# A convolution in a transformed domain: where the second group of weights is prepared

## The chip, the cores and the metric

The kernel runs on one core of one Trainium2 chip. The metric is the device time of one execution in microseconds. Five runs of the kernel before gave 278.68, 279.45, 279.50, 281.03 and 282.76 us; their median, 279.5 us, is the time before.

## The reference

The reference is a circular convolution of an image of 224 x 224 pixels with 96 channels by a 7 x 7 filter with 96 input and 96 output channels, written with Fourier transforms:

```
x: (1, 224, 224, 96) bf16, w: (7, 7, 96, 96) bf16
wp = pad(w) to 224 x 224
Xf = rfft2(x over h, w);  Wf = rfft2(wp over h, w)
Yf = einsum('bhwi,hwio->bhwo', Xf, Wf)
y  = irfft2(Yf).astype(bf16)
```

The product over the channels for each output pixel is what has to be computed; the transforms of the reference are one way to it.

## The kernel before

**The work.** The image's rows are cut into 8 blocks of 28 rows, and within each block the kernel uses a short transform over 34 points (28 rows plus 6 of overlap), which has 17 frequencies. Along the width there is no transform but a direct convolution with 7 taps, folded into 10 (`NTAP`). The width is cut into 7 strips of 32 columns, `t` = 0 to 6. For each strip there are three stages: the forward transform of the image (tile `xf`, matmuls with the matrix `Fm`), a channel product for each frequency `s` (tile `WF` holds the transformed weights, tile `J` holds sums and differences of `xf`), and the transform back (`c_jobs`).

**The weights.** `WF` has one to three parts of 96 x 10 x 96 numbers for each frequency. They are made once, in six groups of frequencies, `PGRP = ((0, 2), (2, 5), (5, 8), ...)`: 12 jobs for a group, each some matmuls of the raw weights (tile `wq`) with a small matrix `Em`, and one copy from PSUM to `WF` (`evac`, by VectorE or ScalarE). For a frequency above 0 the matmuls make two parts, and a subtraction on VectorE, `diff(s)` in line 392, makes the third: it reads the outputs of all 12 jobs of its group.

The raw weights come from memory twice. The first copy fills every second partition of `wq`; the second copy, shifted by 48 output channels, fills the partitions between them. With the first copy alone a matmul makes one output channel (`first_prep`, line 345: 96 matmuls of 50 columns for group 0). With both, one matmul makes two output channels (`prep_jobs`, line 361: 48 matmuls of 120 columns for every other group). The loads of the second copy, `load_w(1, ...)` and `load_wl(1, ...)`, write partitions that the matmuls of the first kind read too, so they wait for the last of these.

**The order.** Every engine gets its instructions in the order in which the program lists them (`_Ordered`, line 77), and so do the transfers that the SP queue issues. The channel products run in rounds: `b_round(t, s, ...)` in line 518 is one frequency of one strip. A round has a first bank of matmuls, a place for other work called `mid`, a second bank of matmuls, subtractions for the tiles `J` in some rounds (`jit`, line 490, on VectorE), and another such place called `end`. These places are the half-rounds. `add(a, b, jobs)` in line 769 spreads a list of jobs evenly over the half-rounds `a` to `b - 1`, and `pace` takes from each list what is due, in the order in which the lists were added. Rounds 0 to 3 work on strip 0 alone, half-rounds 0 to 7; from round 4 on, strip 1 runs beside strip 0, four frequencies behind. Subtractions of `jit` stand in round 1 (frequencies 3 to 5 of strip 0), round 3 (0 to 2 of strip 1) and round 4 (6 to 8 of strip 0).

Before the rounds come the forward transform of the parts that are needed first, group 0's 12 jobs (lines 732 to 742), and the issue of the second weight copy (lines 743 and 744). In the rounds, group 1's 12 jobs all stand in half-round 3, its first `diff` behind them, and its other two in half-rounds 4 and 6. Group 2's jobs are spread over half-rounds 4 to 8. The first part of strip 1's forward transform (`f_jobs(1, 0)`, 8 jobs of 8 matmuls of 64 columns) is spread over half-rounds 0 to 2, its second part over half-rounds 7 to 13, and a rest of strip 0's over half-rounds 0 to 3.

PSUM has 8 banks here, and every job and every round's two banks take one in turn.

Of the kernel before, what the change touches and what calls it, by code (L numbers as in the profile page):

```python
# [25 lines left out]
NB = 8  # L26
POS = TW + HALO
NTAP = 10
TAPS = ((7, 8, 9, 6), (0, 2, 4, 6), (1, 3, 5))
NSLOT = 2 + 3 * (NS - 1)  # L30
PGRP = ((0, 2), (2, 5), (5, 8), (8, 11), (11, 14), (14, 17))
# [16 lines left out]
def slot(s, part):  # L48
    return part if s == 0 else 2 + 3 * (s - 1) + part
# [3 lines left out]
def kernel(  # L53
# [7 lines left out]
    _, H, W, C = x.shape  # L61
# [7 lines left out]
    PW2 = 2 * PW  # L69
# [28 lines left out]
    VE, SE, GE, TE, DE = (_Ordered(e) for e in (nc.vector, nc.scalar, nc.gpsimd, nc.tensor, nc.sync))  # L98
# [9 lines left out]
    def bank():  # L108
        return pools["psb"].tile([128, 512], F32, name="pb")

    load = {"v": 0.0, "a": 0.0, "p": 0.0}
# [3 lines left out]
    def apart(key, zone, r):  # L115
        for z, q in parts.setdefault(key, []):
            if z != zone and q.engine != r.ins.engine:
                tc.declare_no_dep(r.ins, q, reason="disjoint parts of one tile")
        parts[key].append((zone, r.ins))
        return r  # L120

    def evac(out_ap, in_ap, n):
        if tail[0]:
            return tail_evac(out_ap, in_ap, n)
        cv, ca = 180 + 1.0 * n, 160 + 0.85 * n
        for k in "va":
            load[k] = max(load[k], load["p"])
        if load["v"] + cv <= load["a"] + ca:
            load["v"] += cv
            return VE.tensor_copy(out=out_ap, in_=in_ap)  # L130
        load["a"] += ca
        return SE.copy(out=out_ap, in_=in_ap)

    def tail_evac(out_ap, in_ap, n):
        tail[0] += 1
        return VE.tensor_copy(out=out_ap, in_=in_ap) if tail[0] % 2 else SE.copy(out=out_ap, in_=in_ap)

    def dma(out_ap, in_ap):
        return DE.dma_start(out=out_ap, in_=in_ap)

    WF = cpool.tile([128, NSLOT, NTAP, C], BF16, name="WF")
# [18 lines left out]
    wqx = wtmp.tile([128, C - 1 + 127 * C + 1], BF16, name="wq")  # L160
    wq = wqx[0:PW2]
    WA = C * C
    WC = WA - C2
    WZ = WA // 3
    Em = wqx[0:PW2, WA:WA + 2 * NSLOT * NTAP].rearrange("p (h a t) -> p h a t", h=2, a=NSLOT)
# [26 lines left out]
    def load_w(h, cuts):  # L192
        for a, b in zip(cuts[:-1], cuts[1:]):
            wld.append(dma(wqx[h:2 * PW - 3 + h:2, a:b], wsrc[0:PW - 1, h * C2 + a:h * C2 + b]))

    def load_wl(h, n):
        wld.append(dma(wqx[2 * PW - 2 + h:2 * PW - 1 + h, 0:n], wsrc[PW - 1:PW, h * C2:h * C2 + n]))
# [7 lines left out]
    def warm(n):  # L205
        pwu = bank()
        for _ in range(n):
            TE.matmul(pwu[:].rearrange("p (a b) -> p a b", a=4), lhsT=wu[:, 0:128], rhs=wur, start=True, stop=True)
# [133 lines left out]

    g_fin = build_g(3)

    def first_prep():
        n = slot(PGRP[0][1], 0)
        q = n * NTAP
        wv = WF[0:C, 0:n].rearrange("i a t o -> i (a t) o")

        def mk_(o0):  # L350
            def f():
                pw = bank()
                pv_ = pw[:, 0:NB * q].rearrange("p (k q) -> p k q", q=q)
                for k in range(NB):
                    o = o0 + k
                    TE.matmul(pv_[:, k], lhsT=wqx[0:PW2 - 1, o:o + 127 * C + 1:C], rhs=Em[0:PW2 - 1, 0, 0:n].rearrange("p a t -> p (a t)"), start=True, stop=True)
                apart(("W", 0), o0, evac(wv[..., o0:o0 + NB], pv_[0:C].rearrange("i k q -> i q k"), NB * q))
            return f
        return [mk_(o0) for o0 in range(0, C, NB)]

# [44 lines left out]
    def new_xf(t, s0=0, s1=NS):  # L405
        xf = xf_bufs[t % 2]
        xf_tiles[t] = xf
        if t > 0:
            prev = xf_tiles[t - 1]
            for ph in range(2):  # L410
                o, i = (v[0:C, ph, :, s0:s1, p:p + HALO, :].rearrange("c r s w j -> c r s (w j)") for v, p in ((xf, 0), (prev, TW)))
                apart(("A", t), ("halo", s0), SE.copy(out=o, in_=i))
                load["a"] += 160 + 0.85 * 2 * (s1 - s0) * HALO * NJ
        return xf
# [35 lines left out]
    def then_load(f, t, jg):  # L450
        def g():
            f()
            if t < NT:
                load_x(t, jg)
        return g
# [11 lines left out]
    def f_jobs(t, part):  # L467
        s0, s1 = SH2[t][part], SH2[t][part + 1]
        n = 2 * (s1 - s0) * JG
        nr = -(-TW * n // 512)  # L470
        e = [-(-TW * i // nr) for i in range(nr + 1)]
        fv = Fm[:, :, s0:s1].rearrange("p r s j -> p r (s j)")

        def mk_(jg, a, b, ph):
            def f():
                pa = bank()
                load["p"] += max(26.0, 0.43 * n) * (b - a)
                for k in range(b - a):
                    i = 2 * (a + k) + ph
                    TE.matmul(pa[:, k * n:(k + 1) * n], lhsT=xbuf(t, jg)[:, i * C:i * C + 128], rhs=fv, start=True, stop=True)  # L480
                xo = xf_tiles[t][0:C, ph, :, s0:s1, HALO + a:HALO + b, jg * JG:(jg + 1) * JG]
                pi = pa[0:C, 0:(b - a) * n].rearrange("c (w r s j) -> c r s w j", r=2, s=s1 - s0, w=b - a)
                return apart(("A", t), (a, jg, ph, part), evac(xo, pi, (b - a) * n))
            return f
        return [[mk_(jg, a, b, ph) for a, b in zip(e[:-1], e[1:]) for ph in range(2)] for jg in range(2)]
# [232 lines left out]
    def queue_c(t):  # L718
        pend.extend((t, *k) for k in LT)
        pump()  # L720
# [5 lines left out]
    fj = [f_jobs(0, p) for p in range(2)]  # L726
# [2 lines left out]
            f()  # L729
    for _ in range(2):  # L730
        warm(5)
    pj = first_prep()
    for f in pj[:6]:
        f()
    for f in fj[0][1]:
# [4 lines left out]
        f()  # L740
    for f in pj[9:]:
        f()
    load_w(1, (0, WC))
    load_wl(1, WC)
    g_fin()
    stmp_cm.__exit__(None, None, None)
    yf_pool = ctx.enter_context(tc.tile_pool(name="yf", bufs=YBUF))
# [21 lines left out]
    def add(a, b, jobs):  # L769
        qs.append([a, b, jobs, len(jobs)])  # L770

    for gi in range(1, len(PGRP)):
        pj, dj = prep_jobs(gi)
        add(*((3, 4) if gi == 1 else (2 * PGRP[gi - 1][0], 2 * PGRP[gi - 1][1] - 1)), pj)
        for i, f in enumerate(dj):
            k = 2 * (PGRP[gi][0] + i) - (1 if gi == 1 and i == 0 else 2)
            add(k, k + 1, [f])
    for t in range(2):
        scr_tiles[t] = dr_pool.tile([TW, NJ, NS, 4 * C], BF16, name="scr")
# [9 lines left out]
    for r in range(NS + LAG):  # L789
        if r == 0:  # L790
            add(0, 4, fj[1][1])
        for p in range(2):
            if r == (0, 3)[p]:
                new_xf(1, SH2[1][p], SH2[1][p + 1])
                fj = f_jobs(1, p)
                if p == 1:
                    for jg in range(2):
                        fj[jg][-1] = then_load(fj[jg][-1], 2, jg)
                add(2 * r + p, 2 * r + (3, 8)[p], fj[0] + fj[1])
        for p in range(3):  # L800
            if r == (9, 14, 17)[p]:
                new_xf(2, SH2[2][p], SH2[2][p + 1])
                fj = f_jobs(2, p)
                if p == 2:
                    for jg in range(2):
                        fj[jg][-1] = then_load(fj[jg][-1], 3, jg)
                add(2 * r, 2 * r + (8, 7, 5)[p], fj[0] + fj[1])
        if r == PGRP[-2][1] + 1:
            assert not any(q[2] for q in qs if q[1] <= 2 * r)
            wtmp_cm.__exit__(None, None, None)  # L810
            t_pool = ctx.enter_context(tc.tile_pool(name="tt", bufs=NTT, side="right"))
            t2_pool = ctx.enter_context(tc.tile_pool(name="tt2", bufs=1, side="right"))
            yo_pool = ctx.enter_context(tc.tile_pool(name="yo", bufs=2, side="right"))
            g_pool = ctx.enter_context(tc.tile_pool(name="gp", bufs=1, side="right"))
            GA = g_pool.tile([KA, 4 * B], BF16, name="GA")
            GB = g_pool.tile([128, 2, 4 * B], BF16, name="GB")
            GE.memset(GA[:], 0.0)
            GE.memset(GB[:], 0.0)
        if r == NS + 3:
            queue_c(0)  # L820
        for t in range(2):
            s = r - LAG * t
            if not 0 <= s < NS:
                continue
            now = bursts.pop((r, t), ())
            now = jit(*now) if now else ()
            both = LAG <= r < NS
            b_round(t, s, fills(qs, 2 * r + (t if both else 0)), fills(qs, 2 * r + (t if both else 1)), False, now)
# [70 lines left out]
    for _ in range(WARM):  # L899
        TE.matmul(live[order[7]].rearrange("p (a b) -> p a b", a=3), lhsT=wu[:, 0:M4], rhs=wu[:].unsqueeze(1).to_broadcast([128, 3, 128]),  # L900
                  start=False, stop=False)
    LF = 4
    for i, (g, q) in enumerate(order):
# [3 lines left out]
        k = i + 8 - LF  # L907
        if 8 <= k < len(order):
            live[order[k]] = first(*order[k])
        if q % 2:  # L910
            w0, o0 = TL * 2 * TW + (q - 1) * 4, (q - 1) % 4 * 4 * C
# [33 lines left out]
```

## Time and profile before

| What | us |
|---|---|
| median of five runs | 279.5 |
| the profiled execution | 280.88 |
| its span in the profile | 279.2 |
| PE busy | 264.1 (95%) |
| DVE busy | 229.9 (82%) |
| ACT busy | 198.6 (71%) |
| matmuls that read `wq` (both kinds) | 336 |

PE is TensorE, PEld its weight loads, DVE VectorE, ACT ScalarE, POOL GpSimd, SP the queue that issues most transfers. The 1.7 us between the profiled execution and its span lie around the first and last instruction. PE counts as busy while a matmul's record lasts; records overlap, so the pace of a row of matmuls is its length, less the length of the last record, over the number less one. The granted clock is that of TensorE; 1.00 is full speed. The time of a line is measured from the start of the span, and "idle before" names what the engine waited for.

### The profile page before, as it was taken

To read this page: it belongs to the slowest core of one execution; us is meant where nothing else is said; L and a number is where in the kernel's file an instruction comes from. 1 tells how busy PE (TensorE), PEld (TensorE's weight loads), DVE (VectorE), ACT (ScalarE), POOL (GpSimd) and SP (SyncE) were. 2 spreads that over 40 slices of the span, in tenths; PEclk is the share of its full clock that TensorE was granted. 3 is DMA by queue.
4 is the path that set the end of the run, shared out by engine and by line. 5 is a ranking of instruction groups with operands and counts; after the bars stand their busy time and mean duration, and the time that the engine had idled before them with its cause. 6 is when DMAs were issued, how large, how long until landed. Compare 5 with 4: busy or idle time off the path is not lost.

```text
span 279.2 us, 12139 instructions
## 1 busy us (share of the span) xinstructions
PE 264.1 (95%) x5123; PEld 243.7 (87%) x5123; DVE 229.9 (82%) x470; ACT 198.6 (71%) x477; POOL 101.7 (36%) x152
## 2 busy tenths in 40 slices
PE   8989799989998999999999999999999999999964
PEld 3779699989998999898999999999999989989642
DVE  6865769998989979987986897789988889899823
ACT  6567777868784566898988869888888865552422
POOL 7820112254454456224234215222422333645100
PEclk9987979999999999999999999999999999999997
DMA  5975013231111279896978477875969843998675
GB/s 146 267 176 131 2 46 106 82 113 45 45 45 45 85 222 211 240 254 178 294 222 241 134 225 222 212 172 158 275 231 191 267 130 112 191 236 237 165 198 155
DMA packets 46355, 46.79 MB, mean 168 GB/s; under 512 B 35322, under 2 KB 37894, under 8 KB 46250
## 3 DMA queue, kind: packets, MB, share of 16 engines
q1 hardware_dynamic: 45836, 44.34, 57.9%
q0 software_dynamic: 464, 1.67, 1.7%
q8 instruction: 40, 0.66, 1.0%
q14 instruction: 15, 0.12, 0.2%
HBM read 24.66 MB, written 21.33 MB: 165 GB/s over the span
## 4 chain that ended last, share of the span: by engine, by line
PE 55%; DVE 21%; issue 7%; DMA 6%; ACT 5%; POOL 3%; SPq 1%; ACTq 0%; DVEq 0%
PE pb L87 55%; DVE J L87 8%; DVE WF L87 4%; DVE v L87 4%; POOL yf L87 3%; DMA WF<-in_x_dram 3%; ACT WF L87 3%; DMA tt<-scr 2%; DVE u L87 2%; DVE yf L87 1%; DMA xf<-scrl 1%; ACT wq L87 1%; SPq L87 1%; DVE yo L87 1%; ACT xf L87 1%
## 5 line engine op out<-in xcount | busy, mean ns | idle before, releaser
L87 PE MATMUL pb<-WF,J 96*128 96x96 bf16 x2898 | 168.7, 207 | 2.5 <-ACT WF L87 1.4
L87 PEld LDWEIGHTS <-J 96*128 96x128 bf16 x2898 | 142.7, 98 | 11.6 <-DVE J L87 1.7
L87 POOL TENSOR_TENSOR yf<-v,u 128x384 bf16<-128x384 f32 x85 | 84.6, 1012 | 147.1 <-issue 89.9
L87 ACT CAST xf<-pb 96x408 bf16<-96x408 f32 (+5 forms) x143 | 66.9, 488 | 8.9 <-PE pb L87 7.1
L87 PE MATMUL pb<-WF,xf 96*128 96x96 bf16 x952 | 61.7, 207 | 3.9 <-DVE WF L87 3.2
L87 DVE TENSOR_TENSOR J<-xf 96x1824 bf16<-96x1824 bf16 (+1 forms) x84 | 59.9, 752 | 0.0
L87 PEld LDWEIGHTS <-xf 96*128 96x128 bf16 x952 | 48.1, 98 | 4.9 <-issue 4.6
L87 PE MATMUL pb<-Fm,xn 118*128 118x136 bf16 (+4 forms) x576 | 44.9, 205 | 0.0
L87 ACT CAST WF<-pb 96x480 bf16<-96x480 f32 (+1 forms) x61 | 30.3, 559 | 5.9 <-PE pb L87 5.9
L87 PE MATMUL pb<-tt,Gm 102*84 102x384 bf16 (+1 forms) x132 | 33.6, 326 | 0.0
L87 PEld LDWEIGHTS <-xn 118*128 118x128 bf16 x576 | 29.6, 99 | 0.1
L87 ACT CAST yo<-pb 84x384 bf16<-84x384 f32 (+1 forms) x61 | 26.4, 481 | 4.1 <-PE pb L87 3.8
L87 ACT CAST J<-pb 84x384 bf16<-84x384 f32 (+1 forms) x61 | 26.5, 484 | 2.4 <-PE pb L87 2.4
L87 PE MATMUL pb<-wq 98*128 98x120 bf16 (+1 forms) x336 | 25.1, 228 | 0.0
L87 DVE TENSOR_TENSOR J<-J 96x912 bf16<-96x912 bf16 (+1 forms) x42 | 25.0, 594 | 0.0
L87 PEld LDWEIGHTS <-wq 98*128 98x128 bf16 (+1 forms) x336 | 23.0, 154 | 0.2
L87 DVE TENSOR_TENSOR WF<-WF 96x960 bf16<-96x960 bf16 x15 | 16.5, 1100 | 0.5 <-ACT xf L87 0.5
L87 PE MATMUL pb<-wu 128*128 128x512 bf16 (+3 forms) x57 | 15.4, 391 | 1.1 <-DVE wu L87 1.1
L87 DVE TENSOR_TENSOR yf<-v,u 128x384 bf16<-128x384 f32 x27 | 15.5, 572 | 0.9
L87 PEld LDWEIGHTS <-Gm 102*84 102x84 bf16 (+1 forms) x132 | 11.5, 117 | 1.7 <-issue 0.6
L87 PEld LDWEIGHTS <-wu 128*128 128x128 bf16 (+3 forms) x57 | 6.6, 117 | 6.5 <-issue 2.2
L87 DVE CAST xf<-pb 96x512 bf16<-96x512 f32 (+4 forms) x17 | 9.6, 590 | 2.8 <-PE pb L87 2.7
(395 smaller groups left out, 240.9 us busy)
## 6 DMA issues: line engine op xcount, KB each, us to landing
scr<-yf SPq DMA_DIRECT2D x30, 288.0 KB
xn<-in_x_dram SPq DMA_DIRECT2D x12, 672.0 KB
tt<-scr SPq DMA_DIRECT2D x24, 336.0 KB
out_dram<-yo SPq DMA_DIRECT2D x12, 252.0 KB
out_dram<-J SPq DMA_DIRECT2D x12, 252.0 KB
tt<-scr SPq DMA_DIRECT2D x6, 288.0 KB
scrl<-yf POOLq DMA_DIRECT2D x5, 288.0 KB, 5.0
WF<-in_x_dram SPq DMA_DIRECT2D x2, 672.0 KB
```

What stands on the lines that cost most here:

```text
L87: r = fn(*a, **k)
```

## The change

Group 1 is made from the single weight copy as well. `first_prep` becomes `single_prep(gi)`, which for group 1 takes the two computed parts of the three frequencies, 60 columns. Its 12 jobs have 8 matmuls and one copy to `WF` each; two stand before round 0, right behind group 0, and the other ten are spread over half-rounds 0 to 2. The loads of the second weight copy are issued behind the last of them. Group 1's first `diff` moves from half-round 3 to half-round 2. Group 2's jobs stand in half-rounds 6 to 8, four in each. The first part of strip 1's forward transform, with the copy of its halo columns, moves from half-rounds 0 to 2 to half-rounds 3 to 6, two jobs in each.

```
-    def first_prep():
-        n = slot(PGRP[0][1], 0)
-        q = n * NTAP
-        wv = WF[0:C, 0:n].rearrange("i a t o -> i (a t) o")
+    def single_prep(gi):
+        s0, s1 = PGRP[gi]
+        q = (slot(s1 - 1, 2) + 1 - slot(s0, 0)) * NTAP if gi == 0 else (s1 - s0) * 2 * NTAP
+        wv = WF[0:C, slot(s0, 0):slot(s1 - 1, 2) + 1]
+        ev = Em[0:PW2 - 1, 0, slot(s0, 0):slot(s1 - 1, 2) + 1]
+        if gi == 0:
+            ev = ev.rearrange("p a t -> p (a t)")
+        else:
+            ev = ev.rearrange("p (s r) t -> p s (r t)", r=3)[:, :, 0:2 * NTAP]
...
+                load["p"] += 60.0 * NB
                 for k in range(NB):
                     o = o0 + k
-                    TE.matmul(pv_[:, k], lhsT=wqx[0:PW2 - 1, o:o + 127 * C + 1:C], rhs=Em[0:PW2 - 1, 0, 0:n].rearrange("p a t -> p (a t)"), start=True, stop=True)
+                    TE.matmul(pv_[:, k], lhsT=wqx[0:PW2 - 1, o:o + 127 * C + 1:C], rhs=ev, start=True, stop=True)
...
-    pj = first_prep()
+    pj = single_prep(0)
+    p1 = single_prep(1)
...
-    load_w(1, (0, WC))
-    load_wl(1, WC)
+    for f in p1[:2]:
+        f()
+    p1_last = p1.pop()
+
+    def p1_end():
+        p1_last()
+        load_w(1, (0, WC))
+        load_wl(1, WC)
+    p1 = p1[2:] + [p1_end]
...
         pj, dj = prep_jobs(gi)
-        add(*((3, 4) if gi == 1 else (2 * PGRP[gi - 1][0], 2 * PGRP[gi - 1][1] - 1)), pj)
+        if gi == 1:
+            pj = p1
+        add(*((0, 3) if gi == 1 else (6, 9) if gi == 2 else (2 * PGRP[gi - 1][0], 2 * PGRP[gi - 1][1] - 1)), pj)
         for i, f in enumerate(dj):
-            k = 2 * (PGRP[gi][0] + i) - (1 if gi == 1 and i == 0 else 2)
+            k = 2 * (PGRP[gi][0] + i) - 2
             add(k, k + 1, [f])
...
-            if r == (0, 3)[p]:
+            if r == (1, 3)[p]:
...
-                add(2 * r + p, 2 * r + (3, 8)[p], fj[0] + fj[1])
+                add(2 * r + 1, 2 * r + (5, 8)[p], fj[0] + fj[1])
```

## The prediction

> **What bounds the kernel now.** I read the page first, then PE's timeline from 12 to 46 us, the stretch that the change touches, then the clock there window by window, then VectorE's timeline. The page:
>
> ```profile
> span 279.2 us, 12139 instructions
> ...
> PE 264.1 (95%) x5123; PEld 243.7 (87%) x5123; DVE 229.9 (82%) x470; ACT 198.6 (71%) x477; POOL 101.7 (36%) x152
> ...
> PEclk9987979999999999999999999999999999999997
> ```
>
> PE is busy nearly throughout, and behind 46 us it hardly rests: from 46 to 255 us it is busy for 206.0 of 209 us. So what PE gains or loses before 46 us reaches the end almost whole, unless VectorE (50.1 of 54 us busy from 46 to 100) holds it back; its lead has to be looked at too. The granted clock falls twice early. PE's timeline (start, length, group, idle before it):
>
> ```profile
> 17.40 3.10 PE L87 MATMUL pb<-wq 97*128 97x50 bf16 x48
> 21.08 0.80 PE L87 MATMUL pb<-WF,xf 96*128 96x96 bf16 x8 [0.58 <-ACT WF L87]
> ...
> 22.40 1.47 PE L87 MATMUL pb<-Fm,xn 118*128 118x64 bf16 x24
> 23.69 1.31 PE L87 MATMUL pb<-WF,J 96*128 96x96 bf16 x14
> ...
> 25.07 0.87 PE L87 MATMUL pb<-Fm,xn 118*128 118x64 bf16 x24
> ...
> 27.98 3.19 PE L87 MATMUL pb<-wq 98*128 98x120 bf16 x48
> ...
> 32.73 0.33 PE L87 MATMUL pb<-WF,J 96*128 96x96 bf16 x4 [1.40 <-ACT WF L87]
> ...
> 33.88 0.33 PE L87 MATMUL pb<-WF,xf 96*128 96x96 bf16 x4 [0.64 <-DVE WF L87]
> ```
>
> Group 1's 48 matmuls start without a wait, but behind them PE waits 1.40 us for their copies to `WF` and 0.64 us for the first `diff`. The clock (columns: busy time and count of PE, PEld, DVE, ACT, POOL, then PEclk):
>
> ```profile
> 14.81:18.22 3.41, 2.62 (x61) 2.54 (x60) 1.88 (x3) 1.98 (x5) 1.22 (x4) 1.00 1.00 235
> 18.22:21.63 3.41, 2.83 (x46) 2.74 (x45) 2.50 (x5) 2.94 (x8) 0.26 (x1) 0.50 0.21 62
> 21.63:25.05 3.42, 3.42 (x59) 3.42 (x57) 1.97 (x3) 1.79 (x5) 0.10 (x1) 0.50 0.96 241
> ...
> 31.87:35.28 3.41, 1.91 (x36) 1.83 (x37) 1.72 (x5) 1.91 (x5) 0.22 (x1) 1.00 0.04 10
> 35.28:38.70 3.42, 3.42 (x45) 3.42 (x43) 1.66 (x4) 2.59 (x7) 0.99 (x1) 0.50 0.01 2
> ```
>
> The clock is halved from 18.22 to 25.05 and from 35.28 to 38.70, always on a raster of 3.41 us. The window ahead of each fall held waits or many short matmuls. What counts seems to be the time in which columns stream: 512 columns take 216 ns (10 such matmuls in 2.32 us), so 0.42 ns a column. By that, 14.81 to 18.22 streamed 0.40 of the time and 31.87 to 35.28 about 0.45; both were followed by a fall. 11.40 to 14.81 streamed 0.54 and was not. At half clock, 18.22 to 21.63 streamed 0.60 and was not released, and 21.63 to 25.05 streamed all the time and was.
>
> **The change part by part.** Paces from the rows (length less last record, over number less one): 50 columns of `wq` 61 ns, 120 columns 63 ns, 64 columns of `xn` 30 ns (53 at half clock), 96 columns of `WF` 42 ns (79 at half clock), 72 columns 33 and 61 ns. The short `wq` matmuls kept 61 ns at both clocks.
>
> 1. PE's added work. 60 columns lie between the 50 and 120 that were measured, so 62 ns: 96 x 62 = 5.95 us for 48 x 63 = 3.02 us: **+2.9 us**, all on PE. The copies to `WF` stay 12 of 480 elements.
>    By the Trainium skill (TensorE: Matmul & The Clock Gate, Back-to-back issue gap) one matmul takes N/2.4 + 2.5 ns, 27.5 and 52.5 ns here, and this term would be +0.1 us; it says there that loads of weights add to this in a stream. The rows say that 50 and 120 columns cost the same.
> 2. Waits removed. Two jobs (16 matmuls, 1.0 us) fill the 0.58 us at 20.5: the last copies of group 0 end at 21.02, the jobs at about 21.3. Group 1's other jobs run beside rounds 0 and 1, one copy per 0.5 us shared by two engines that take 0.47 (ACT, 9 in 4.25 us) and 0.59 us (DVE, 3 in 1.77 us). The 1.40 and 0.64 us go: **-2.6 us** together.
> 3. What is late next. I followed the built order with these durations. PE reaches the end of round 0's first bank at 21.95, round 1 at 27.15, its last short matmul at 29.6, round 2 at 31.0, round 3 at 33.4. The first `diff` is ready at 30.85, before its use at 31.4. But on VectorE the J subtractions of round 1 (1.95 us by the row at 29.00 and the next) now stand behind it: 31.8 to 33.75. Behind them are a u and `diff(3)`, ready at 34.7, or at 35.2 if POOL's sum beside it slows it (0.65 us alone, 1.40 at 43.69 with POOL at work). PE wants it at 33.7: **+1.3 us** of new wait (bounds 1.0 to 1.5). Queued behind it are the rest of round 3 and group 2's jobs.
> 4. The second copy. Its loads move from 20.5 to 29.6 on SP, past nothing: SP's next transfer waits until 38.04 for a finished sum. Transfers ran until about 25.8, 5.3 us behind the issue; so it is there at 34.9 or up to a microsecond later, and half-round 6 wants it at 35.5. **+0.2 us** (bounds 0 and 3.5; the upper end from the first copy, issued from 3.12 and first read at 12.61, 9.5 us).
> 5. The moved transform. Its 8 jobs cost what they did; all 8 copies but one stand on ACT, which ends them at 34.85, then two halo copies, and round 3's scaled copy at 36.3. VectorE then has u, a `diff`, two copies to `WF`, one to `xf`, v, and the J subtractions for strip 1 from 39.5 to 41.5, against 41.56 to 43.5 before. Half-round 7 takes banks that u and these copies free, in time. `diff(5)` is ready at 43.9 instead of 45.1, PE's 0.46 us of wait there nearly goes (**-0.4 us**), and VectorE leads by 2 us. Cost of this move: nothing, with that lead as its cover; without it the 0.46 us stay.
> 6. First stretch of half clock. 22 matmuls of 96, 12 of 72 and 24 of 64 columns lost 22 x 37 + 12 x 28 + 24 x 23 ns = 1.7 us. Now 32 short matmuls, which lose nothing, fill 2.0 us of it: 13 of 96 and 12 of 72 lose 0.8 us. **-0.9 us**.
> 7. Second stretch. 30 matmuls of 96 columns and some 10 of `wq` lost 30 x 37 + 10 x 36 ns = 1.5 us. It followed the waits of part 2. In part 3 the wait is shorter, and the window streams some 0.5, which by the numbers above may go either way: **-1.5 us**, or 0.
>
> Sum: 2.9 - 2.6 + 1.3 + 0.2 - 0.4 - 0.9 - 1.5 = -1.0 us: a profiled execution of 279.9 instead of 280.88 us. Of that gain 2.4 us are clock. The five runs spread by 4.1 us and their median lies 1.4 us under the profiled execution, so the median one need not have had both falls. With all of the clock terms the median would be 278.5, with half of them 279.7; I take **279.0 us**, no change within 1%, which is about what a measurement of this kernel can tell from none.
>
> The Trainium skill (same page, What's actually happening) has a free-running window of 3413 ns, a fall after an idle one and a release after a busy one. The raster is in the trace; but the window ahead of 35.28 was not idle, PE worked for 1.91 us of it. By that rule the rival below could not happen.
>
> **The rivals.**
>
> *The clock stays halved (slower).* Short matmuls at half clock stream 50 of 62 ns. With 32 of them the window 21.63 to 25.05 streams 0.86 of the time, between 0.60 (not released) and 1.0 (released). If that is not enough, the next two windows with 24 each aren't either, and PE runs at half clock until 35.3: 61 matmuls of 96, 20 of 72 and 16 of 64 columns lose 61 x 37 + 20 x 28 + 16 x 23 ns = 3.2 us, of which the wait in part 3 hides 1.3. 279.0 + 1.9 = 280.9 us, and 282.2 without that cover. For it speaks the 0.60 row; against it that 0.86 is nearer to 1. It decides from the point at which a window with three in five matmuls short is not released.
>
> *The clock is released early and nothing waits (faster).* The two jobs at 20.3 raise the window 18.22 to 21.63 to about 0.73; if that releases at 21.63, 0.8 us more go, and if `diff(3)` is ready in time, 1.3 us more, with the 0.2 of the copy 2.3 in all: 278.5 - 2.3 = 276.2 us. Against it: J and `diff(3)` are in one queue.
>
> *The second copy lands late (slower).* If it takes the first copy's 9.5 us, PE waits 3.3 us more in half-round 6, and the clock falls behind it: 282.3 us. Against it: the first copy shared the queues with the image (DMA share 1.00 ahead of 18.22), this one has them alone (0.04 from 31.87 to 35.28).
>
> That the change doesn't do what it says is out: the built order has 16 short matmuls ahead of round 0, then 32, 24 and 24, and group 2 in three lots of 16 from half-round 6 on.
>
> **How the numbers follow.** Forecast 0.58, clock halved 0.20, early release 0.13, late copy 0.09. Half of the early release lies under 276.7, with 0.04 of the forecast: faster by over 1% 0.10. A third of the clock's rival and half of the copy's lie over 282.3: slower 0.11; within 1% 0.79. The range leaves out the lower part of the early release and the tops of the slower two: 276.5 to 281.8 us.
>
> **What would show it.** After: `wq` matmuls of 60 columns at about 62 ns; no wait for ACT's `WF` near 21 and 31 us; a wait for DVE's `WF` of some 1.3 us near 34; the first 120-column matmul near 35.5 to 36, with or without a wait for a DMA; full clock from 25 on. The prediction is wrong if short matmuls pace at half of 62 ns, if the clock is 0.50 past 25, or if the lead at 45 us is lost before 100 us in VectorE's queue.

## The result

Of the kernel before 71 runs now have a median of 279.27 us, of the changed one 36 runs have 278.85 us; the ratio is **0.9992, with a 95% interval of 0.9977 to 1.0007** (runs over 1.5% above a kernel's fastest are left out of every ratio here). The forecast was 279.0 us and no change within 1%. The time is right, the sum behind it only in part: its clock term for the first stretch failed, its new wait was too large, its price for the moved transform tells too little, and one of the rivals came about as well.

The profiled execution took 278.41 us, 2.5 us less than that of before. That is more than the change did. VectorE's last subtraction for `J` ahead of 97 us starts at 96.23 us instead of 96.94, so 0.7 us were won by then; the rest lies behind it. From 270 to 275 us the execution of before ran at a mean clock of 0.66, that of the changed kernel at 1.00.

The page of the changed kernel, with the same lines as before:

```profile
span 276.7 us, 12237 instructions
...
PE 265.6 (96%) x5171; PEld 245.4 (89%) x5171; DVE 229.8 (83%) x469; ACT 199.7 (72%) x478; POOL 101.8 (37%) x152
...
PEclk9996699999999999999999999999999999999998
```

PE has 48 matmuls more, and the clock has one low stretch ahead of 40 us instead of two. PE's timeline over the changed stretch:

```profile
17.09 4.06 PE L87 MATMUL pb<-wq 97*128 97x50 bf16 x64
...
21.32 2.13 PE L87 MATMUL pb<-wq 97*128 97x60 bf16 x32
23.28 0.90 PE L87 MATMUL pb<-Fm,WF 118*128 118x72 bf16 x12
23.98 1.31 PE L87 MATMUL pb<-WF,J 96*128 96x96 bf16 x14
25.10 1.64 PE L87 MATMUL pb<-wq 97*128 97x60 bf16 x24
...
28.36 1.65 PE L87 MATMUL pb<-wq 97*128 97x60 bf16 x24
...
35.90 0.33 PE L87 MATMUL pb<-WF,xf 96*128 96x96 bf16 x4 [0.32 <-DVE WF L87]
...
36.72 1.20 PE L87 MATMUL pb<-wq 98*128 98x120 bf16 x16 [0.19 <-DMA wq<-in_w_dram]
```

The three waits of before (0.58, 1.40 and 0.64 us) are gone; two small ones have come, for the second subtraction of group 1 (0.32 us) and for the second weight copy (0.19 us). The clock by windows of 3.41 us (busy time and count of PE, PEld, DVE, ACT, POOL, then the clock):

```profile
19.14:22.55 3.41, 3.41 (x63) 3.41 (x61) 2.20 (x4) 3.22 (x9) 0.38 (x1) 1.00 0.15 37
22.55:25.96 3.41, 3.41 (x56) 3.41 (x55) 1.78 (x3) 1.76 (x5) 0.00 (x0) 0.50 0.00 0
25.96:29.38 3.42, 3.42 (x54) 3.42 (x53) 1.02 (x4) 2.58 (x6) 0.00 (x0) 0.50 0.02 5
29.38:32.79 3.41, 3.41 (x58) 3.41 (x56) 2.70 (x6) 2.14 (x5) 0.00 (x0) 0.50 0.54 134
32.79:36.20 3.41, 3.09 (x83) 2.98 (x80) 3.41 (x6) 3.23 (x8) 1.00 (x1) 1.00 0.54 139
```

PE was busy all the time and yet ran at half clock for three windows: two with records of 30 short matmuls each, and a third with 11, behind which the full clock came back. This is the rival "the clock stays halved". It is no accident of the profiled execution: the mean granted clock of the 36 executions lies between 0.954 and 0.980, that of the 12 executions of a1_wide below, with one such window in its trace, between 0.988 and 0.998.

### The profile page after: what moved, and what is told of

It is laid out like the page before. It is cut to its first block, busy times and chain, and to the rows that moved or that the text cites. A ratio compares the mean times of both kernels' runs of the same rounds, so it can differ in the third digit from the quotient of the medians.

```text
span 276.7 us, 12237 instructions
## 1 busy us (share of the span) xinstructions
PE 265.6 (96%) x5171; PEld 245.4 (89%) x5171; DVE 229.8 (83%) x469; ACT 199.7 (72%) x478; POOL 101.8 (37%) x152
## 4 chain that ended last, share of the span: by engine, by line
PE 60%; DVE 21%; issue 7%; POOL 4%; DMA 4%; ACT 2%; SPq 1%; DVEq 0%; ACTq 0%; POOLq 0%
PE pb L87 60%; DVE J L87 8%; DVE WF L87 4%; POOL yf L87 4%; DVE v L87 4%; DMA xf<-scrl 3%; DVE u L87 2%; DVE yf L87 1%; ACT xf L87 1%; DMA scrl<-yf 1%; SPq L87 1%; DVE yo L87 0%; ACT WF L87 0%; DVE xf L87 0%; DVE tt L87 0%
## 5 line engine op out<-in xcount | busy, mean ns | idle before, releaser
L87 ACT CAST xf<-pb 96x408 bf16<-96x408 f32 (+5 forms) x145 | 68.1, 490 | 8.0 <-PE pb L87 6.0
L87 PE MATMUL pb<-wq 98*128 98x120 bf16 (+2 forms) x384 | 27.6, 227 | 0.2 <-DMA wq<-in_w_dram 0.2
L87 PEld LDWEIGHTS <-wq 97*128 97x128 bf16 (+1 forms) x384 | 25.6, 158 | 0.5 <-DMA wq<-in_w_dram 0.3
L87 DVE CAST WF<-pb 96x480 bf16<-96x480 f32 (+1 forms) x12 | 7.3, 622 | 4.6 <-PE pb L87 4.6
```

What stands on the lines that cost most here:

```text
L87: r = fn(*a, **k)
```

## The experiments

### Short matmuls that stream twice their columns (a1_wide)

```
-                    TE.matmul(pv_[:, k], lhsT=wqx[0:PW2 - 1, o:o + 127 * C + 1:C], rhs=ev, start=True, stop=True)
+                    po, rv = pv_[:, k], ev
+                    if gi == 0 or k < NB - 1:
+                        po = pw[:, k * q:(k + 2) * q]
+                        rv = ev.unsqueeze(1).to_broadcast([PW2 - 1, 2, *ev.shape[1:]])
+                    TE.matmul(po, lhsT=wqx[0:PW2 - 1, o:o + 127 * C + 1:C], rhs=rv, start=True, stop=True)
```

Of the eight matmuls of a job of group 1 the last stays at 60 columns, so 84 of the 96 are wide, and all 96 of group 0.

> The changed kernel, in which each of the 192 short matmuls streams its columns twice (100 and 120 columns; the second lot is overwritten by the next matmul, so the result stays the same). Their pace should stay at 61 to 63 ns, the weights' load. Theory 'columns hold the clock': the granted clock stays 1.00 from 19 to 36 us where the changed kernel's profile had 0.50 from 22.55 to 32.79; PE wins 3 us there, the wait for the second subtraction of group 1 (0.32 us in the changed kernel) grows to about 1.3 us, and the time falls by some 1.5 to 2 us, ratio to the kernel before 0.993. Rival 'VectorE has the stretch anyway': the clock stays, the waits grow by as much as PE wins, ratio 0.999. Rival 'waits set the clock': the clock falls all the same near 22 us, ratio 0.999 or above.

Measured: 278.05 us (12 runs; the kernel before beside it 279.11), ratio 0.9981 (0.9949 to 1.0013). PE's timeline and the clock by windows:

```profile
26.23 1.61 PE L87 MATMUL pb<-wq 97*128 97x120 bf16 x24
...
32.79 0.33 PE L87 MATMUL pb<-WF,xf 96*128 96x96 bf16 x4 [0.70 <-DVE WF L87]
...
34.80 1.49 PE L87 MATMUL pb<-wq 98*128 98x120 bf16 x16 [1.39 <-DMA wq<-in_w_dram]
```

```profile
21.66:25.07 3.41, 3.41 (x69) 3.41 (x68) 1.81 (x3) 2.48 (x6) 0.00 (x0) 1.00 0.00 0
25.07:28.49 3.42, 3.42 (x77) 3.42 (x75) 1.59 (x4) 3.16 (x8) 0.00 (x0) 1.00 0.02 5
...
31.90:35.31 3.41, 1.32 (x25) 1.07 (x22) 2.39 (x5) 2.00 (x6) 2.49 (x2) 1.00 0.14 39
35.31:38.73 3.42, 3.42 (x48) 3.42 (x47) 2.42 (x4) 1.69 (x4) 0.00 (x0) 0.50 0.22 86
```

120 columns keep the pace (24 in 1.61 us as against 1.64), and the clock now stays whole until 35.31: how many columns stream decides it here, with no wait removed and no matmul more. But the time hardly falls. PE is early now and waits 0.70 us for the subtraction and 1.39 us for the second copy, both in one window, and the clock falls behind that one. Counted from group 0's first matmul, both kernels reach the same 18 matmuls on `J` at the same time (43.12 - 12.62 = 30.50 us here, 43.60 - 13.06 = 30.54 us in the changed kernel). So the stretch at half clock had been hidden: without it these two waits and the later fall take its place.

### The same with half of group 1's matmuls (a2_half)

```
-                for k in range(NB):
+                for k in range(0, NB, 1 if gi == 0 else 2):
```

This kernel leaves out every second output channel of group 1, and so half of its matmuls.

> As a1_wide, but group 1's jobs have 4 matmuls of 120 columns instead of 8: every second output channel of group 1 is left out (it gets the neighbour's values). Against a1_wide this takes away the 48 matmuls that the change added and nothing else. If they cost what the prediction charged, 3.0 us less of PE ahead of round 2, and 3.0 us less time where PE sets the pace: ratio to the kernel before about 0.983. If VectorE sets the pace from round 1 to round 5, most of it comes back as wait for WF, and the ratio is that of a1_wide.

Measured: 274.84 us beside 278.05 us of a1_wide on the same chip, 3.2 us less; ratio 0.9898 (0.9854 to 0.9942). That is near what the prediction charged for the 48 added matmuls (2.9 us), but the difference is not their price alone, though the expectation takes it so: the copy is issued earlier too, PE waits 0.19 us for it instead of 1.39, the fall at 35.31 does not come, and PE waits 0.86 and 0.18 us for subtractions instead of 0.70. The price itself is read from the rows: 24 matmuls of 60 columns in 1.64 us are a pace of 62 ns, 3.0 us for 48.

### The second subtraction ahead of J (a3_wide_diff3)

```
-            k = 2 * (PGRP[gi][0] + i) - 2
+            k = 2 * (PGRP[gi][0] + i) - (4 if gi == 1 and i == 1 else 2)
```

> As a1_wide, with the second subtraction of group 1 moved from half-round 4 to half-round 2, so that it stands ahead of round 1's J subtractions in VectorE's queue. If that queue order is what makes PE wait in round 3, the wait of about 1.3 us for DVE's WF near 33 us goes, and the time falls by up to 1 us against a1_wide, since J comes 0.65 us later. If it is J itself that round 3 waits for, nothing is won.

Measured: 278.08 us, ratio 1.0003 (0.9978 to 1.0028), as a1_wide. PE's timeline in round 3:

```profile
33.31 0.50 PE L87 MATMUL pb<-WF,xf 96*128 96x96 bf16 x8
33.65 0.47 PE L87 MATMUL pb<-WF,J 96*128 96x96 bf16 x7
36.30 1.81 PE L87 MATMUL pb<-wq 98*128 98x120 bf16 x16 [2.19 <-DMA wq<-in_w_dram]
```

The 8 matmuls that were cut in two by the wait now run in one piece, so the order in VectorE's queue was its cause. Nothing is won: the wait for the copy is 2.19 instead of 1.39 us. Behind the subtraction the copy is the next late thing.

### The kernel before with wide matmuls (b_wide)

```
-                    TE.matmul(pv_[:, k], lhsT=wqx[0:PW2 - 1, o:o + 127 * C + 1:C], rhs=Em[0:PW2 - 1, 0, 0:n].rearrange("p a t -> p (a t)"), start=True, stop=True)
+                    ev = Em[0:PW2 - 1, 0, 0:n].rearrange("p a t -> p (a t)")
+                    TE.matmul(pw[:, k * q:(k + 2) * q], lhsT=wqx[0:PW2 - 1, o:o + 127 * C + 1:C],
+                              rhs=ev.unsqueeze(1).to_broadcast([PW2 - 1, 2, q]), start=True, stop=True)
```

> The kernel before, in which the 96 short matmuls of group 0 stream their 50 columns twice, result unchanged. Theory 'columns hold the clock': the half-clock stretch that its profile had from 18.22 to 25.05 is gone, PE wins 1.7 us ahead of group 1's matmuls, which then may wait for the second weight copy (there at 26 to 27 us, first read at 27.98), so 0.7 to 1.7 us less, ratio 0.995. If the waits near 16 and 20.5 us set the clock, it falls as before, ratio 1.000.

Measured: 277.98 us (beside 279.11), ratio 0.9991 (0.9959 to 1.0024): by the ratio no gain, though the half-clock stretch ahead of 25 us is gone (the clock is 1.00 up to 33.40 us, then 0.50 for one window). PE now reaches group 1 before the second copy does (0.40 us of wait), and the wait of 1.45 us for group 1's copies to `WF` stays:

```profile
26.62 3.14 PE L87 MATMUL pb<-wq 98*128 98x120 bf16 x48 [0.40 <-DMA wq<-in_w_dram]
...
31.38 0.33 PE L87 MATMUL pb<-WF,J 96*128 96x96 bf16 x4 [1.45 <-ACT WF L87]
```

### Group 2 back in half-rounds 4 to 8 (c1_grp2_early)

```
-        add(*((0, 3) if gi == 1 else (6, 9) if gi == 2 else (2 * PGRP[gi - 1][0], 2 * PGRP[gi - 1][1] - 1)), pj)
+        add(*((0, 3) if gi == 1 else (2 * PGRP[gi - 1][0], 2 * PGRP[gi - 1][1] - 1)), pj)
```

> The changed kernel with one part undone: group 2's jobs back in half-rounds 4 to 8. PE reaches half-round 4 near 33.5 us, the second copy was in the changed kernel's profile there at 36.7. Theory 'the copy is on the path': PE waits some 3 us for the copy there, the clock falls behind it, 2 to 3 us more than the changed kernel, ratio to the kernel before 1.008. Rival 'VectorE hides it': the wait takes the place of the wait for WF, the ratio stays at 0.999.

Measured: 282.89 us beside 279.20, ratio 1.0175 (1.0135 to 1.0215).

```profile
36.15 1.42 PE L87 MATMUL pb<-wq 98*128 98x120 bf16 x12 [2.84 <-DMA wq<-in_w_dram]
```

The wait has the size expected, and nothing hides it. The price, 1.8% or 5 us over the changed kernel where 2 to 3 were expected, is more than the wait: this execution was at half clock again from 35.9 to 42.7 us, two windows.

### Strip 1's transform back in half-rounds 0 to 2 (c2_fwd_early)

```
-            if r == (1, 3)[p]:
+            if r == (0, 3)[p]:
...
-                add(2 * r + 1, 2 * r + (5, 8)[p], fj[0] + fj[1])
+                add(2 * r + p, 2 * r + (3, 8)[p], fj[0] + fj[1])
```

> The changed kernel with one part undone: the first part of strip 1's forward transform back in half-rounds 0 to 2, ahead of and between the short matmuls. Its 64 matmuls of 64 columns (30 ns each at full clock, 53 at half) then delay the last short matmul and with it the second copy by 1.9 to 3.4 us, while PE has as much less to do before half-round 6: the wait for the copy grows from 0.2 us to 2 us or more, ratio 1.005. If the prediction was right that the move itself costs and wins nothing, the ratio differs from 0.999 by that wait alone; if the lead of VectorE by the earlier J for strip 1 matters, it is 0.999 or less in spite of the wait.

Measured: 281.07 us beside 279.20, ratio 1.0095 (1.0058 to 1.0132). The price is larger than expected (1.005), and the place is another. There is no wait for the copy at all:

```profile
34.33 0.34 PE L87 MATMUL pb<-WF,J 96*128 96x96 bf16 x4 [0.93 <-DVE J L87]
...
36.52 0.48 PE L87 MATMUL pb<-WF,xf 96*128 96x96 bf16 x4 [1.68 <-DVE WF L87]
```

VectorE's timeline says why:

```profile
32.87 1.40 DVE L87 TENSOR_TENSOR J<-xf 96x1824 bf16<-96x1824 bf16 x2
34.19 0.62 DVE L87 TENSOR_TENSOR J<-J 96x912 bf16<-96x912 bf16 x1
...
35.01 1.47 DVE L87 TENSOR_TENSOR WF<-WF 96x960 bf16<-96x960 bf16 x1
```

Without the transform's matmuls in half-rounds 4 and 5, PE comes to round 3 while VectorE is still at round 1's J, and waits 2.6 us for J and the subtraction behind it; the clock then was 0.50 from 35.76 to 42.58. In the changed kernel the moved matmuls are what PE does meanwhile. One copy of the transform (0.68 us at 31.81) also stands ahead of J on VectorE here; that can be 0.7 of the 2.6 us at most, and the rest was not split further.

### The moves without the new group 1 (c4_moves_only)

```
-        add(*((3, 4) if gi == 1 else (2 * PGRP[gi - 1][0], 2 * PGRP[gi - 1][1] - 1)), pj)
+        add(*((3, 4) if gi == 1 else (6, 9) if gi == 2 else (2 * PGRP[gi - 1][0], 2 * PGRP[gi - 1][1] - 1)), pj)
...
-            if r == (0, 3)[p]:
+            if r == (1, 3)[p]:
...
-                add(2 * r + p, 2 * r + (3, 8)[p], fj[0] + fj[1])
+                add(2 * r + 1, 2 * r + (5, 8)[p], fj[0] + fj[1])
```

> The kernel before with the moves alone: group 2 in half-rounds 6 to 8 and the first part of strip 1's transform in 3 to 6, group 1 as before with 48 matmuls of both copies in half-round 3. PE then has 64 matmuls of 64 columns less ahead of group 1 and comes to it at about 25 us, 1 to 2 us before the second copy is there (26 to 27), and behind group 1 the waits of 1.40 and 0.64 us for WF stay: ratio about 1.003. If the gain of the change were in the moves, it would be below 0.999.

Measured: 278.98 us beside 279.20, ratio 1.0010 (0.9971 to 1.0049). The profiled execution is the slowest of the twelve:

```profile
26.79 4.99 PE L87 MATMUL pb<-wq 98*128 98x120 bf16 x48 [2.44 <-DMA wq<-in_w_dram]
```

```profile
23.36:26.78 3.42, 0.98 (x26) 0.86 (x23) 2.52 (x6) 1.22 (x4) 0.00 (x0) 1.00 0.45 113
26.78:30.19 3.41, 3.40 (x35) 3.41 (x36) 1.26 (x3) 2.77 (x6) 1.02 (x1) 0.50 0.03 7
```

PE waits 2.44 us for the second copy ahead of group 1, whose 48 matmuls then take 4.99 us at half clock. The moves alone win nothing that can be measured.

### Wide matmuls and a later group 2 (c3_wide_grp2_late)

The edit of a1_wide, and this:

```
-        add(*((0, 3) if gi == 1 else (6, 9) if gi == 2 else (2 * PGRP[gi - 1][0], 2 * PGRP[gi - 1][1] - 1)), pj)
+        add(*((0, 3) if gi == 1 else (7, 10) if gi == 2 else (2 * PGRP[gi - 1][0], 2 * PGRP[gi - 1][1] - 1)), pj)
...
-            k = 2 * (PGRP[gi][0] + i) - 2
+            k = 2 * (PGRP[gi][0] + i) - (1 if gi == 2 and i == 0 else 2)
```

> a1_wide with group 2's jobs in half-rounds 7 to 9 instead of 6 to 8, and the first subtraction of group 2 in half-round 9. In a1_wide PE waited 1.39 us for the second copy at half-round 6 and the clock was 0.50 for the window behind. If that wait is what ate the gain of the full clock, both go: 1 to 2 us less than a1_wide, ratio to the kernel before 0.993. If VectorE's queue ate it, the wait comes back as wait for WF in round 5, ratio 0.998.

Measured: 276.06 us (7 runs between 274.86 and 276.62) beside 279.20, **ratio 0.9922 (0.9890 to 0.9954)**. PE's timeline and the clock:

```profile
32.75 0.33 PE L87 MATMUL pb<-WF,xf 96*128 96x96 bf16 x4 [0.70 <-DVE WF L87]
34.70 1.20 PE L87 MATMUL pb<-wq 98*128 98x120 bf16 x16 [0.25 <-DMA wq<-in_w_dram]
```

```profile
31.79:35.20 3.41, 2.46 (x56) 2.21 (x53) 2.64 (x7) 2.52 (x7) 2.50 (x2) 1.00 0.14 39
35.20:38.62 3.42, 3.42 (x78) 3.42 (x77) 3.01 (x6) 3.42 (x9) 0.57 (x1) 1.00 0.25 91
```

The copy lands when it did in a1_wide, but PE does round 3's second bank first, and of 1.39 us of wait 0.25 are left. The clock never falls in this stretch. So that wait, with the fall behind it, was where the full clock's gain had gone. This kernel beats both.

### The two halves of it (d1_grp2_late and d2_wide1_grp2_late)

d1 is the changed kernel with the later group 2 alone:

```
-        add(*((0, 3) if gi == 1 else (6, 9) if gi == 2 else (2 * PGRP[gi - 1][0], 2 * PGRP[gi - 1][1] - 1)), pj)
+        add(*((0, 3) if gi == 1 else (7, 10) if gi == 2 else (2 * PGRP[gi - 1][0], 2 * PGRP[gi - 1][1] - 1)), pj)
...
-            k = 2 * (PGRP[gi][0] + i) - 2
+            k = 2 * (PGRP[gi][0] + i) - (1 if gi == 2 and i == 0 else 2)
```

> The changed kernel with group 2's jobs in half-rounds 7 to 9 and its first subtraction in 9, the matmuls left short: c3_wide_grp2_late without its wide matmuls. If c3's gain (ratio 0.992) is the clock's, this keeps the half-clock stretch of three windows from about 22 us and comes out near the changed kernel, ratio 0.998 to 1.000, since that waited only 0.19 us for the copy. If the gain is in the later place of group 2, it comes near 0.993.

Measured: 278.54 us beside 279.46, ratio 0.9957 (0.9925 to 0.9989), between the two answers and too wide to choose; it overlaps c3's and the change's. The trace has 0.50 for four windows from 20.24 to 33.90, and no wait for the copy.

d2 is c3_wide_grp2_late with group 0's matmuls short again:

```
-                    if gi == 0 or k < NB - 1:
+                    if gi == 1 and k < NB - 1:
```

> c3_wide_grp2_late with group 0's matmuls short again and group 1's wide. If the columns that stream decide, group 0's 6 us at 21 of 61 ns still let the clock fall near 18 to 22 us; then 120 columns fill their pace at half clock (99 ns instead of 63) and the clock is back after one window: a half-clock stretch of 3.4 us instead of none, ratio 0.994 to 0.998. If any wide matmuls will do, it is 0.992.

Measured: 275.66 us (6 runs) beside 279.46, ratio 0.9875 (0.9817 to 0.9933), no worse than c3. In the profiled execution the clock did not fall behind group 0, and five of the six executions have a mean clock of 0.996 or more:

```profile
19.12:22.54 3.42, 3.42 (x60) 3.42 (x60) 2.03 (x4) 3.22 (x8) 0.37 (x1) 1.00 0.01 4
```

d1 and d2 ran beside each other and differ only in the columns of group 1's matmuls: 278.54 and 275.66 us, 2.9 us. So it is group 1's columns that matter, and c3's gain needs them together with the later group 2; neither wins as much alone (0.9981 in a1_wide, 0.9957 in d1). The expected fall is a miss. In the changed kernel's profile, too, the windows of group 0 alone (from 12.31 and 15.72, streaming 0.46 and 0.49 of the time by the count of the last section) were not followed by one; it came behind the next window, from 19.14 (0.45), and there d2 streams 0.69.

## Why the prediction was right, and where it was not

*1. PE's added work.* Right: the short matmuls of the changed kernel pace at 62 ns, 3.0 us for 48, and a2_half without them is 3.2 us faster. The Trainium skill's formula for a matmul by itself (TensorE: Matmul & The Clock Gate, Back-to-back issue gap) gives an estimate of 0.1 us. By a1_wide it is not what counts here, since 120 columns cost as much time as 60.

*2. Waits removed.* Right: 0.58, 1.40 and 0.64 us are gone in the changed kernel's timeline.

*3. What is late next.* The mechanism was right, the size not. The subtraction behind J took 1.39 us beside POOL's sum, the upper of the two durations:

```profile
34.46 1.39 DVE L87 TENSOR_TENSOR WF<-WF 96x960 bf16<-96x960 bf16 x1
```

(By that duration of 1.40 the prediction's upper bound should have been near 1.7: ready at 35.45, not 35.2.) But PE waited 0.32 us and not 1.3, because it came late itself, at half clock. With the full clock of a1_wide, where the subtraction took 0.65 us, the wait is 0.70 us, still under the lower bound of 1.0. a3 shows that the queue's order makes it.

*4. The second copy.* The wait was 0.19 us for 0.2, partly by luck. From the end of the last short matmul, near 30.0, to the first read it took 6.7 us where I had 5.3 and up to a microsecond more; PE's late arrival covered the difference. At full clock it was 1.39 us, and in c1 2.84 us.

*5. The moved transform.* The 0.46 us of wait at 45 us is gone, as forecast, though VectorE's J for strip 1 starts at 40.46 us, 1.1 us earlier than before and not 2. What failed is the account: "Cost of this move: nothing", with VectorE's lead as its cover. Undone in c2 the change is 1.0% slower (1.0095 for 0.9992), 2.9 us, so the move is a condition of the other terms. I had looked at what its copies delay and not at what its matmuls cover: they are PE's work while VectorE does J and the subtraction.

*6 and 7. The clock.* Term 6 failed: the half-clock stretch was not cut short by the short matmuls but became longer, 10.2 us instead of 6.8. The prediction's own sign of being wrong, a clock of 0.50 past 25 us, came about. Term 7 held: no fall at 35 us. The rival had priced the longer stretch at 3.2 us, less what the wait in part 3 hides. The cover was larger than that, since the copy hides too: lifting the clock in a1_wide showed waits of 2.1 us where there had been 0.5, and a fall behind them. So a case that the prediction set at 281 us came about at no loss.

In sum, group 1 by 96 matmuls costs 3 us, takes 2.6 us of waits away and brings 0.5 us of new ones; the two moves are needed to keep it from losing 1 to 2% (c1, c2) and win nothing alone (c4). That is the "no change" of the forecast. That its time came out so close is partly luck. By the prediction's own prices the three windows at half clock lost some 3.0 us (an estimate: 47 matmuls of 96, 32 of 72 and 16 of 64 columns) against 1.7 before, so term 6 was +1.3 and not -0.9 us, 2.2 us off one way; the wait of part 3 was 1.0 us off the other way, and the forecast stood 0.5 us over the 278.5 of the sum.

## What to carry to other kernels

A stretch at half clock is worth only what the next wait behind it leaves: take the wait and the clock together (c3 won 0.8% against the kernel before, the wide matmuls alone 0.2% with an interval that holds no change). Where the pace of a row of matmuls does not depend on its columns (here 61 to 63 ns from 50 to 120 columns at full clock), columns are free, and twice the columns can keep the clock up. Before a job is moved, ask what the engine will do in the place that it leaves, not only what it delays in the new one.

## What the runs showed of the hardware

- **PE can be busy and still be throttled.** With records over 3.41 of 3.41 us, two windows of the changed kernel were not released from half clock. Counting columns at 0.42 ns (0.83 at half clock), half-clock windows that streamed 0.91 to 0.93 of the time were not released (in the changed kernel and c1), those with 0.97 to 1.0 were (c2, a1_wide and others), and 0.94 went both ways (released in the kernel before at 270.81, not in d1 at 27.07). One window speaks against the count: c4's from 26.78 streamed all the time by it and was not released. The Trainium skill has a release after one busy window (TensorE: Matmul & The Clock Gate, What's actually happening). Here that holds only if busy means streaming columns, and in c4's window not even then.
- **The fall is less clear.** At full clock, every window under 0.40 was followed by a fall, and none over 0.47. Between them some were, as in the kernel before (0.41 and 0.46), and some with 0.41 to 0.47 were not (d1 at 13.42, c4 at 13.12 and 16.54, d2 at 12.30). What else counts was not found.
- **The spread of the times goes with the clock.** Of the kernel before, the 20 executions beside c1 to c4 run from 276.73 us at a mean granted clock of 0.992 over 279.36 us at 0.976 to 283.41 us at 0.961.
- **With wide matmuls the spread was narrower.** 12 executions of a1_wide lay between 276.56 and 278.91 us, 12 of b_wide between 276.54 and 279.72 us, and 29 of the kernel before beside them between 276.50 and 283.20 us.
